# Projection matmuls grouped in threes over six PSUM banks, at the border between two token blocks

## The chip, the cores and the metric

One NeuronCore of a Trainium2 chip runs the program. The metric is the device time of one execution in microseconds (us); the kernel before was run three times and its median is what the changed kernel is held against. The engines are TensorE (PE in the profile, its weight loads PEld), VectorE (DVE), ScalarE (ACT), GpSimd (POOL) and SyncE (SP). Matmul results land in PSUM, eight banks of 128 partitions by 512 fp32.

## What is computed

A cross attention between `x` and a small `state` gives 4,352 token rows of 512 numbers; these go through a mixture of eight experts in which every expert sees every token, weighted by a matrix `P` that eight rounds of row and column normalisation make:

```
xread = softmax(scale * x @ state.T) @ state          # per batch b and head h, 512 tokens
sread = softmax(scale * state @ x.T) @ x              # 32 state rows
x     = concat(xread, sread) reshaped to (4352, 512)
for e in range(8):
    h   = max(x @ w1[e], 0)                           # 512 -> 1024
    out += P[:, e:e+1] * (h @ w2[e])                  # 1024 -> 512
```

## The kernel before

**Blocks.** The tokens are cut into nine blocks: eight of 512 tokens (one for each batch entry) and a ninth, block 8, with the 256 state rows. A first part of the program (some 140 us) computes the attention, the matrix `P` and expert 0, in an order that a small planner (`issue`, L48) writes. The rest is a loop (L858 on) over the 63 pairs of expert 1 to 7 and block 0 to 8; its order is written out by hand, and it is what the change touches. Each pair is called a block below, and written (expert, block).

**The first layer.** For a block of 512 tokens `x @ w1` is not computed from `x`. Its rows are attention weights times `state`, so `V = state @ w1` is computed first (`project`, L192, "projection"), and `hidden_ps` (L210) multiplies the attention weights `aT` by `V`. A projection of one block has two halves of 512 columns. A half is 8 matmuls that each use a 64x32 piece of the array (`tile_position`), so that all 8 stand side by side; they fill two PSUM banks, and ScalarE copies these to `V` (L208). `V` lives in a ring of three buffers. `layer1` (L226) then makes eight steps for a block; a step is one bank `hps` from two matmuls of 512 columns, which ScalarE turns into `Hm` with a relu (L238). After the fourth and the eighth step VectorE forms four sums and differences of `Hm` (L244 to L247, called S1 and S2 below). Block 8 takes its `x` from `xsT` directly, in four matmuls of 256 columns a step.

**The second layer.** `layer2` (L257) replaces the eight quarter products of `h @ w2` by seven (a Strassen scheme). Each of the seven products is 8 matmuls of 256 columns (4 in block 8), all on line 271. They go to three PSUM tiles, in this order, with k counting from 0:

- k=0: `A`; ScalarE copies it to the block's `Bseed` bank (L305)
- k=1: `E`; k=2: onto `Bseed`; k=3: onto `A`; k=4: onto `Bseed`; k=5: onto `E`; k=6: onto `Bseed`
- after each from k=1 on, VectorE adds the tile, times a column of `P`, to `acc` (`add`, L281, two instructions on L285; one in block 8). A product onto a tile waits until the add that reads the tile's former state has ended.

Two `Bseed` banks alternate between blocks.

**PSUM in the loop.** Eight banks: `A`, `E`, two `Bseed`, and a ring of four named "h", which the `hps` steps and the projections share.

**The order in the loop.** Between the products of a block come the steps of the *next* block's first layer: none after k=0 and k=1, then 1, 2, 2, 2, 1. After k=0 stands the projection of the block after the next one, both halves, wherever there is one to make: in 54 of the 63 blocks. At every sixth call of `step` a piece of the next expert's weight preparation is issued (`load_w`, L160: loads on GpSimd's queue, then eight differences `T` on VectorE, L178). In expert 1, GpSimd also multiplies `acc` by a column of `P` for each block (`weigh`, L250).

All engines run their own instructions in order, so the place at which an instruction is written in this loop is its place in its engine's queue.

Of the kernel before, what the change touches and what calls it, by code (L numbers as in the profile page):

```python
# [9 lines left out]
FP32 = mybir.dt.float32  # L10
FP16 = mybir.dt.float16
AX_X = mybir.AxisListType.X
ALU = mybir.AluOpType
AF = mybir.ActivationFunctionType
EPS = 1e-9


class Ring:
# [71 lines left out]
def kernel(  # L90
# [9 lines left out]
    nc = tc.nc  # L100
# [32 lines left out]
    def bank(shape, dtype, name, tag="bank"):  # L133
        return pools[tag].tile(shape, dtype, name=name, tag=tag)
# [20 lines left out]

    mw = ctx.enter_context(tc.tile_pool(name="moe_w", bufs=2))
    gsb = ctx.enter_context(tc.tile_pool(name="gate_sb", bufs=2))
    vpool = ctx.enter_context(tc.tile_pool(name="vpool", bufs=3))

    def load_w(e):  # L160

        w1h = mw.tile([128, NKC, F], FP16, name="w1h", tag="w1h")
        w2h = mw.tile([128, NFB, Dm], FP16, name="w2h", tag="w2h")
        w16[e] = (w1h, w2h)
        for g in range(2):
            nc.gpsimd.dma_start(out=w1h[:, ds(2 * g, 2), :], in_=w1r[e, :, ds(2 * g, 2), :])  # L166
        for g in range(2):
            nc.gpsimd.dma_start(out=w2h[:, ds(NJ * g, NJ), :], in_=w2r[e, :, ds(NJ * g, NJ), :])
        for _ in range(10):
            yield  # L170
        T = tpool[0].tile([128, 4, NJ, DH], FP16, name="T", tag="T")
        tsum[e] = T
        b11, b12 = w2h[:, :NJ, :DH], w2h[:, :NJ, DH:]
        b21, b22 = w2h[:, NJ:, :DH], w2h[:, NJ:, DH:]
        for i, (p, q) in enumerate(((b12, b11), (b22, T[:, 0]), (b22, b12), (b21, T[:, 1]))):
            for g in range(2):
                jj = ds(g * (NJ // 2), NJ // 2)
                nc.vector.tensor_sub(T[:, i, jj], p[:, jj], q[:, jj])  # L178
                yield
# [9 lines left out]
    asb = actx.enter_context(tc.tile_pool(name="attn_sb", bufs=2))  # L189
    spl = actx.enter_context(tc.tile_pool(name="stprep", bufs=1))  # L190

    def project(e, bi):  # L192
        if bi == B:
            return
        w1h = w16[e][0]
        V = vpool.tile([128, NQ, F], FP16, name="V", tag="V")
        vt[(e, bi)] = V
        for f in range(F // 512):
            cols = ds(f * 512, 512)
            ps = [bank([128, 512], FP32, "v_ps", ring[0]) for _ in range(NQ)]  # L200
            for j in range(4):
                for q in range(NQ):
                    r = ((j ^ q) % 2) * 64
                    nc.tensor.matmul(ps[q][ds(j * Ns, Ns), :], stT[ds(r, 64), bi, q, ds((j ^ q) * Ns, Ns)],  # L204
                                     w1h[ds(r, 64), 2 * q + j // 2, cols],
                                     tile_position=(r, j * Ns))
            for q in range(NQ):
                nc.scalar.copy(out=V[:, q, cols], in_=ps[q])  # L208

    def hidden_ps(e, bi, fb, out):  # L210
        w1h = w16[e][0]
# [7 lines left out]
            nc.tensor.matmul(out, lhs, rhs, start=(k == 0), stop=(k == len(terms) - 1))  # L219

    vt = {}
    ring = ["bank"]
    hid = {}
    seeds = []

# [31 lines left out]
    def layer2(e, bi, n):  # L257
        t0, tn = blocks[bi]
        nk = tn // 256
        th = tn // 2  # L260
        Hm, sm = hid.pop((e, bi))
        w2h, T = w16[e][1], tsum[e]
        tb = t0 // 128
        p = Pmat[:, :, e:e + 1]
        A = bank([128, 2, DH], FP32, "A", "A")
        Eb = bank([128, 2, DH], FP32, "E", "E")

        def product(dst, lhs, rhs, first=False):
            for c in range(nk):
                for j in range(NJ):  # L270
                    nc.tensor.matmul(dst[:, c], lhs(j, c), rhs[:, j],  # L271
                                     start=first and c == 0 and j == 0, stop=(j == NJ - 1),
                                     skip_group_check=True)

        def h(i, half):
            return lambda j, c: Hm[:, i, j, ds(half * th + c * 128, 128)]

        def s(k):
            return lambda j, c: sm[:, k, j, ds(c * 128, 128)]

        def add(src, row, col):  # L281
            for c in range(nk):
                k = tb + row * nk + c
                dst = acc[:, k, ds(col * DH, DH)]
                nc.vector.scalar_tensor_tensor(out=dst, in0=src[:, c], scalar=p[:, k], in1=dst,  # L285
                                               op0=ALU.mult, op1=ALU.add)

        def store(row):
            if e == E - 1 and bi == B:
                nb = 128 // Ns  # L290
                for i in range(nb):
                    (nc.scalar if i % 2 else nc.sync).dma_start(
                        out=outs[row * nb + i], in_=acc[ds(i * Ns, Ns), tb + row, :])

        if e == 1:
            for b in range(2) if bi == 0 else (bi + 1,):
                weigh(b)
        product(A, h(0, 0), w2h[:, :NJ, :DH], True)
        if not n:
            for i in range(2):  # L300
                bb = pb.tile([128, 2, DH], FP32, name="Bseed%d" % i)
                nc.tensor.matmul(bb.rearrange("p c d -> p (c d)"), identh, aT[:, 0, 0], start=True, stop=True)
                seeds.append(bb)
        Bb = seeds[n % 2]
        nc.scalar.copy(out=Bb[:, :nk], in_=A[:, :nk])  # L305
        yield
        product(Eb, s(0), T[:, 0], True)
        add(Eb, 1, 1)
        yield
        product(Bb, s(1), T[:, 1])  # L310
        add(Bb, 0, 1)
        yield
        product(A, h(1, 0), w2h[:, NJ:, :DH])
        add(A, 0, 0)
        yield
        product(Bb, h(0, 1), T[:, 2])
        add(Bb, 1, 1)
        yield
        product(Eb, s(2), w2h[:, NJ:, DH:])
        add(Eb, 0, 1)  # L320
        store(0)
        yield
        product(Bb, h(1, 1), T[:, 3])
        add(Bb, 1, 0)
        if e == E - 1 and bi < B:
            for k in range(2 * nk):
                nc.sync.dma_start(out=outx[bi][:, k, :], in_=acc[:, tb + k, :])
        store(1)
        yield
# [18 lines left out]
    def slot(pool, n, shape, dtype, tag):  # L348
        return Slot(rings.setdefault(tag, Ring(n)),
                    lambda: pool.tile(shape, dtype, name=tag, tag=tag))  # L350
# [333 lines left out]
    vslots = {}  # L684

    def project_ops(e, b, rank):
        V = slot(vpool, 3, [128, NQ, F], FP16, "V")
        vslots[e, b] = V
        outs_ = []
        for f in range(F // 512):  # L690
            cols = ds(f * 512, 512)
            ps = [psum([128, 512], FP32, "v_ps") for _ in range(NQ)]

            def mul(_, ps=ps, cols=cols):
                w1h = wslots[e][0].tile
                for j in range(4):
                    for q in range(NQ):
                        rr = ((j ^ q) % 2) * 64
                        nc.tensor.matmul(ps[q].tile[ds(j * Ns, Ns), :],  # L699
                                         stT[ds(rr, 64), b, q, ds((j ^ q) * Ns, Ns)],  # L700
                                         w1h[ds(rr, 64), 2 * q + j // 2, cols],
                                         tile_position=(rr, j * Ns))

            t = op(rank, {"PE": (0.40, 0.62)}, mul, stT_ready + w1_ready(e) + ([t] if f else []), ps + ([] if f else [V]), [V] if f else [])
            for q in range(NQ):
                def keep(eng, q=q, ps=ps, cols=cols):
                    copy(eng, V.tile[:, q, cols], ps[q].tile)
                    vt[e, b] = V.tile

                outs_.append(op(rank, EVICT32, keep, [t], [], [ps[q], V]))  # L710
        v_ready[e, b] = outs_
# [131 lines left out]
    for tag in ("A", "E"):  # L843
        pools[tag] = ctx.enter_context(
            tc.tile_pool(name="psum_" + tag, bufs=1, space=bass.MemoryType.PSUM))
    ring[0] = "h"
    n = 0

    def step():
# [6 lines left out]
                wload.pop(0)  # L856

    work = [(e, bi) for e in range(1, E) for bi in range(len(blocks))]  # L858
    for i, (e, bi) in enumerate(work):
        if bi == 1 and e + 1 < E:  # L860
            wload.append(load_w(e + 1))
        l2 = layer2(e, bi, i)
        l1 = layer1(*work[i + 1]) if i + 1 < len(work) and work[i + 1] not in hid else iter(())
        for k in range(7):
            next(l2)
            step()
            if k == 0 and i + 2 < len(work) and work[i + 2] not in vt:
                project(*work[i + 2])
            for _ in range((0, 0, 1, 2, 2, 2, 1)[k]):
                next(l1, None)  # L870
                step()
        for part in (l1, l2):
            for _ in part:
                pass
        if bi == len(blocks) - 3:
            for _ in (x for w in wload for x in w):
                pass
            wload.clear()
# [30 lines left out]
```

## Time and profile before

| | us |
|---|---|
| three runs: median (lowest to highest) | 768.05 (767.78 to 769.49) |
| the profiled execution's own time | 766.84 |
| its span, first to last instruction | 764.9 |
| TensorE busy | 747.9 (98%) |
| VectorE busy | 629.9 (82%) |
| ScalarE busy | 513.7 (67%) |
| GpSimd busy | 104.6 (14%) |

The profile is one execution. Its lines give an engine, a source line, the operation, what it writes and reads, the shape, a count, and times; the idle time before an instruction is given with what ended it. The end of a matmul is modelled and includes the way through the array, so matmuls that follow each other overlap in the listing: eight products of 256 columns are listed as 1.04 us and start 0.87 us before the next group. The chain view follows the last instruction back to what released it, step by step, and gives each group only the time that it adds.

### The profile page before, as it was taken

The numbers are of one execution on the slowest core, as the hardware profiler recorded it, in microseconds if no ns is written. First come the engines' busy times: TensorE is split into PE (matmuls) and PEld (weight loads), VectorE is DVE, ScalarE is ACT, GpSimd is POOL, SyncE is SP. The second block draws the span as 40 slices with busy tenths as digits, with TensorE's granted clock in tenths as the row PEclk, the third lists the DMA queues.
The fourth block names the chain that finished last, engine by engine and source line by source line (L and its number), as shares of the span: only waits on it lengthen the run. The fifth ranks groups of instructions, "written<-read, shape, count | busy, mean of one in ns | idle before, by whom it ended". The sixth has DMA issues, their size and how long they took to land.

```text
span 764.9 us, 16309 instructions
## 1 busy us (share of the span) xinstructions
PE 747.9 (98%) x6561; PEld 501.8 (66%) x6561; DVE 629.9 (82%) x1544; ACT 513.7 (67%) x1003; POOL 104.6 (14%) x102
## 2 busy tenths in 40 slices
PE   5999999999999999999999999999999999999997
PEld 3444445566776667766776767766677667766775
DVE  5998977888987888888887888888887888878886
ACT  5878976666667675766657666676657676576662
POOL 4433100799200000100001000100001000000000
PEclk9999999999999999999999999999999999999999
DMA  8997200060015000510006000240006000012234
GB/s 136 184 152 120 49 1 1 1 112 1 1 25 88 1 2 1 91 21 2 1 1 111 2 1 1 44 69 1 2 1 108 4 2 1 1 55 86 85 108 138
DMA packets 41595, 34.61 MB, mean 45 GB/s; under 512 B 16688, under 2 KB 33072, under 8 KB 41520
## 3 DMA queue, kind: packets, MB, share of 16 engines
q0 software_dynamic: 21248, 20.97, 17.7%
q1 hardware_dynamic: 19040, 12.08, 6.4%
q8 instruction: 51, 0.84, 0.4%
q10 hardware_dynamic: 1232, 0.52, 0.3%
q14 instruction: 24, 0.20, 0.1%
HBM read 42.48 MB, written 8.91 MB: 67 GB/s over the span
## 4 chain that ended last, share of the span: by engine, by line
PE 90%; DVE 5%; ACT 3%; DMA 1%; issue 0%; POOL 0%; POOLq 0%
PE hps L219 27%; PE Bseed L271 20%; PE E L271 14%; PE A L271 13%; PE yps L756 7%; PE v_ps L204 4%; PE hps L721 4%; DVE acc L285 2%; DMA x_nat<-in_x_dram 1%; DVE sm L244 1%; ACT V L357 1%; ACT Hm L238 1%; PE su_ps L596 1%; PE v_ps L699 0%; ACT xT L357 0%; PE ET_ps L581 0%
## 5 line engine op out<-in xcount | busy, mean ns | idle before, releaser
L238 ACT ACTIVATE Hm<-hps 128x512 f16<-128x512 f32 (+1 forms) x496 | 266.0, 572 | 188.5 <-PE hps L219 173.4
L219 PE MATMUL hps<-aT,V 128*128 128x512 f16 x880 | 234.8, 379 | 0.0
L271 PEld LDWEIGHTS <-Hm 128*128 128x128 f16 x1904 | 186.2, 98 | 69.8 <-issue 0.8
L285 DVE SCALAR_TENSOR_TENSOR acc<-Bseed,Pmat,acc 128x256 f32<-128x256 f32 x357 | 156.9, 479 | 56.9 <-PE Bseed L271 54.4
L271 PEld LDWEIGHTS <-sm 128*128 128x128 f16 x1428 | 134.2, 98 | 52.5 <-DVE sm L244 24.2
L271 PE MATMUL Bseed<-T,Hm 128*128 128x256 f16 x952 | 124.5, 273 | 0.4 <-DVE acc L285 0.3
L271 PE MATMUL A<-w2h,Hm 128*128 128x256 f16 x952 | 124.7, 273 | 0.0
L219 PEld LDWEIGHTS <-V 128*128 128x128 f16 x880 | 86.1, 98 | 45.2
L208 ACT CAST V<-v_ps 128x512 f16<-128x512 f32 x216 | 111.3, 610 | 0.0
L285 DVE SCALAR_TENSOR_TENSOR acc<-E,Pmat,acc 128x256 f32<-128x256 f32 x238 | 104.3, 477 | 3.7
L244 DVE TENSOR_TENSOR sm<-Hm 128x512 f16<-128x512 f16 (+1 forms) x124 | 51.7, 417 | 19.1 <-ACT Hm L238 18.3
L756 PE MATMUL yps<-w2h,hT 128*128 128x512 f16 x272 | 66.5, 380 | 0.0
L285 DVE SCALAR_TENSOR_TENSOR acc<-A,Pmat,acc 128x256 f32<-128x256 f32 x119 | 52.4, 479 | 15.8 <-PE A L271 15.7
L271 PE MATMUL E<-T,sm 128*128 128x256 f16 x476 | 64.5, 274 | 0.7
L271 PE MATMUL Bseed<-T,sm 128*128 128x256 f16 x476 | 62.4, 273 | 0.0
L271 PE MATMUL E<-w2h,sm 128*128 128x256 f16 x476 | 62.3, 273 | 0.0
L254 POOL TENSOR_SCALAR acc<-acc,Pmat 128x512 f32<-128x512 f32 x34 | 55.2, 1638 | 44.8 <-DVE Pmat L673 44.8
L166 POOL DMA_DIRECT2D w1h<-in_moe_w_dram x12 | 8.6, 721 | 355.2 <-PE hps L219 355.2
L247 DVE TENSOR_TENSOR sm<-Hm,sm 128x512 f16<-128x512 f16 (+1 forms) x124 | 53.1, 428 | 4.2
L245 DVE TENSOR_TENSOR Hm<-Hm 128x512 f16<-128x512 f16 (+1 forms) x124 | 51.6, 416 | 4.3
L246 DVE TENSOR_TENSOR sm<-sm,Hm 128x512 f16<-128x512 f16 (+1 forms) x124 | 50.0, 403 | 0.0
L305 ACT COPY Bseed<-A 128x512 f32<-128x512 f32 (+1 forms) x63 | 34.4, 546 | 18.8 <-PE A L271 17.3
(107 smaller groups left out, 554.1 us busy)
## 6 DMA issues: line engine op xcount, KB each, us to landing
w1h<-in_moe_w_dram POOLq DMA_DIRECT2D x16, 512.0 KB, 7.2
w2h<-in_moe_w_dram POOLq DMA_DIRECT2D x16, 512.0 KB, 7.5
out_dram<-acc SPq DMA_DIRECT2D x32, 256.0 KB, 2.8
x_nat<-in_x_dram POOLq DMA_DIRECT2D x16, 256.0 KB, 6.3
st_st<-in_state_dram SPq DMA_DIRECT2D x1, 256.0 KB, 4.2
st_st<-in_state_dram ACTq DMA_DIRECT2D x1, 256.0 KB, 4.6
out_dram<-acc SPq DMA_DIRECT2D x4, 64.0 KB, 1.9
out_dram<-acc ACTq DMA_DIRECT2D x4, 64.0 KB, 2.1
```

Of the source, the lines that this page charges most:

```text
L208: nc.scalar.copy(out=V[:, q, cols], in_=ps[q])
L219: nc.tensor.matmul(out, lhs, rhs, start=(k == 0), stop=(k == len(terms) - 1))
L238: nc.scalar.activation(out=Hm[:, i, j, :tn], in_=hps[:, :tn], func=AF.Relu)
L244: nc.vector.tensor_add(s1, a21, a22)
L245: nc.vector.tensor_sub(a21, a11, a21)
L246: nc.vector.tensor_sub(s2, s1, a11)
L247: nc.vector.tensor_sub(s4, a12, s2)
L254: nc.gpsimd.tensor_scalar(out=acc[:, k, :], in0=acc[:, k, :], scalar1=Pmat[:, k, 0:1], scalar2=None, op0=ALU.mult)
L271: nc.tensor.matmul(dst[:, c], lhs(j, c), rhs[:, j], start=first and c == 0 and j == 0, stop=(j == NJ - 1), skip_group_check=True)
L285: nc.vector.scalar_tensor_tensor(out=dst, in0=src[:, c], scalar=p[:, k], in1=dst, op0=ALU.mult, op1=ALU.add)
L305: nc.scalar.copy(out=Bb[:, :nk], in_=A[:, :nk])
L756: nc.tensor.matmul(yps.tile, hT[fb].tile[:, ds(tk * 128, 128)], w2h[:, fb, :], start=(fb == 0), stop=(fb == NFB - 1))
```

## The change

`project` now takes a list of three halves, which may belong to two blocks, and the block's number, and does its work as a generator in two parts. Its 24 matmuls are issued in one go. The first half goes to the `E` bank and to the `Bseed` bank of the block that follows; the other two go to the four "h" banks. ScalarE's copies of the first two banks are issued with the matmuls, those of the other four at the second call.

The loop calls it ahead of `layer2` of block i, so the matmuls stand between product k=6 of the block before and product k=0 of this one; the other four copies come after k=0, behind the copy of `A` to `Bseed`. A session is made only where the next block's `V` is not complete, which gives 36 sessions of three halves for the 54 of two. The steps of the first layer get other places: the string PAT with a session, PAT0 without, PATN in block 7 and PATS in block 8 (without a session). In all of them no step comes after k=6, and the fourth step comes before k=4.

```diff
+PAT = (0, 0, 1, 3, 2, 2, 0)
+PAT0 = (0, 1, 1, 2, 2, 2, 0)
+PATN = (1, 1, 1, 2, 2, 1, 0)
+PATS = (1, 1, 1, 1, 2, 2, 0)
+VB = 3
...
-    def project(e, bi):
-        if bi == B:
-            return
-        w1h = w16[e][0]
-        V = vpool.tile([128, NQ, F], FP16, name="V", tag="V")
-        vt[(e, bi)] = V
-        for f in range(F // 512):
+    def project(halves, n):
+        banks = []
+        for k, (e, bi, f) in enumerate(halves):
+            if (e, bi) not in vt:
+                vt[(e, bi)] = vpool.tile([128, NQ, F], FP16, name="V", tag="V")
+            w1h = w16[e][0]
             cols = ds(f * 512, 512)
-            ps = [bank([128, 512], FP32, "v_ps", ring[0]) for _ in range(NQ)]
+            if k:
+                ps = [bank([128, 512], FP32, "v_ps", "h") for _ in range(NQ)]
+            else:
+                ps = [bank([128, 512], FP32, "v_ps", "E"), seeds[n % 2].rearrange("p c d -> p (c d)")]
             for j in range(4):
                 for q in range(NQ):
                     r = ((j ^ q) % 2) * 64
                     nc.tensor.matmul(ps[q][ds(j * Ns, Ns), :], stT[ds(r, 64), bi, q, ds((j ^ q) * Ns, Ns)],
                                      w1h[ds(r, 64), 2 * q + j // 2, cols],
                                      tile_position=(r, j * Ns))
-            for q in range(NQ):
-                nc.scalar.copy(out=V[:, q, cols], in_=ps[q])
+            banks += [(vt[(e, bi)][:, q, cols], ps[q]) for q in range(NQ)]
+        for dst, src in banks[:2]:
+            nc.scalar.copy(out=dst, in_=src)
+        yield
+        for dst, src in banks[2:]:
+            nc.scalar.copy(out=dst, in_=src)
+        yield
...
+    halves = [(e, bi, f) for e, bi in work if bi < B and (e, bi) not in vt for f in range(F // 512)]
     for i, (e, bi) in enumerate(work):
         if bi == 1 and e + 1 < E:
             wload.append(load_w(e + 1))
+        v = iter(())
+        pat = PATS if bi == B else PATN if bi == B - 1 else PAT0
+        if i + 1 < len(work) and (work[i + 1] + (F // 512 - 1,)) in halves:
+            v = project(halves[:3], i)
+            pat = PAT
+            del halves[:3]
+        next(v, None)
         l2 = layer2(e, bi, i)
         l1 = layer1(*work[i + 1]) if i + 1 < len(work) and work[i + 1] not in hid else iter(())
         for k in range(7):
             next(l2)
             step()
-            if k == 0 and i + 2 < len(work) and work[i + 2] not in vt:
-                project(*work[i + 2])
-            for _ in range((0, 0, 1, 2, 2, 2, 1)[k]):
+            if k == 0:
+                next(v, None)
+            for _ in range(pat[k]):
                 next(l1, None)
                 step()
```

More of the change, by code (lines that the diff above doesn't have):

```diff
@@ L157 @@
     gsb = ctx.enter_context(tc.tile_pool(name="gate_sb", bufs=2))
-    vpool = ctx.enter_context(tc.tile_pool(name="vpool", bufs=3))
+    vpool = ctx.enter_context(tc.tile_pool(name="vpool", bufs=VB))
     def load_w(e):
@@ L221 @@
     vt = {}
-    ring = ["bank"]
     hid = {}
@@ L686, in project_ops @@
     def project_ops(e, b, rank):
-        V = slot(vpool, 3, [128, NQ, F], FP16, "V")
+        V = slot(vpool, VB, [128, NQ, F], FP16, "V")
         vslots[e, b] = V
@@ L845 @@
             tc.tile_pool(name="psum_" + tag, bufs=1, space=bass.MemoryType.PSUM))
-    ring[0] = "h"
     n = 0
```

## The prediction, made before the changed kernel was run

> **What bounds the kernel now.** I read the page first, then TensorE's busy time by windows, the chain, the timeline of some blocks, and the order of the instructions of both programs on each engine.
>
> ```profile
> PE 747.9 (98%) x6561; PEld 501.8 (66%) x6561; DVE 629.9 (82%) x1544; ACT 513.7 (67%) x1003; POOL 104.6 (14%) x102
> 300.00:450.00 150.00, 149.92 (x1303) 106.28 (x1302) 123.98 (x309) 101.40 (x195) 5.83 (x8) 1.00 0.17 29
> ```
>
> In the loop TensorE is busy 149.92 of 150 us at a granted clock of 1.00 (the second line: PE, PEld, DVE, ACT, POOL, clock). So only TensorE's own time, or a new wait of TensorE, can move the end. Its time at a projection, in the chain:
>
> ```profile
> 303.20 0.87 PE A L271 x8
> 304.07 0.56 PE v_ps L204 x16
> 304.63 0.98 PE E L271 x8
> ```
>
> A product costs 0.87 us; a session of two halves costs 0.56 and makes the next product 0.11 longer, together 0.67 (0.66 from the starts). A half streams 512 columns through eight pieces side by side, 0.215 us, as one matmul of 512 columns does (four `hps` matmuls: 0.86). So 0.66 - 0.43 = 0.23 us a session is spent on going into and out of the small pieces.
>
> **Fewer sessions.** 54 sessions become 36, the 108 halves stay: 18 x 0.23 = **4.1 us less**. That the 0.23 belongs to the session and not to its matmuls, the first part shows, where a single half stands between products:
>
> ```profile
> 112.65 1.02 PE L756 MATMUL yps<-w2h,hT 128*128 128x512 f16 x4
> 113.60 0.41 PE L699 MATMUL v_ps<-w1h,stT 64*32 64x512 f16 x8
> 113.95 1.04 PE L756 MATMUL yps<-w2h,hT 128*128 128x512 f16 x4
> ```
>
> Four matmuls end their streaming at 112.65 + 0.86 = 113.51, the next group starts at 113.95: 0.44 for one half, 0.22 of it fixed. From below, the saving could be nothing (a rival).
> A rule of the Trainium skill speaks against it: "TensorE: Matmul & The Clock Gate", section "The cost: per-tile semaphore tail", lets the tail grow with the packed matmuls and their semaphore increments. By its formula the tail would be an estimated 0.21 us for 16 matmuls with 4 increments and 0.30 for 24 with 6, so 54 and 36 of them would cost nearly the same. The trace doesn't agree: 0.22 after 8 matmuls, 0.23 after 16.
>
> **Waits that go.** Where a block has no session (block 6 of each expert), the last step of the first layer stands right before k=0, and S2 comes too late for k=1:
>
> ```profile
> 294.09 1.29 PE L271 MATMUL E<-T,sm 128*128 128x256 f16 x8
> ```
>
> 1.29 against 1.04: 0.25 us, in six experts; in (7,6) and (7,7) 0.23 each. All steps now end before k=6, so S2 has 0.87 us more. With three small ones (0.2): **2.2 us less**. In (7,8) a wait of 0.3 for S2 goes, but the next two waits for adds take its place; nothing.
>
> **Waits that come: S1.** The order shows what the diff hides: the fourth step now comes before k=4, so on VectorE S1 stands ahead of the add of k=4, which before was ahead of S1. Product k=6 waits for that add. The parts, from the timeline:
>
> ```profile
> 299.76 1.08 ACT L238 ACTIVATE Hm<-hps 128x512 f16<-128x512 f32 x2 [0.65 <-PE hps L219]
> 300.39 0.42 DVE L244 TENSOR_TENSOR sm<-Hm 128x512 f16<-128x512 f16 x1 [0.18 <-ACT Hm L238]
> 301.99 0.42 DVE L178 TENSOR_TENSOR T<-w2h,T 128x512 f16<-128x512 f16 x1
> ```
>
> S1 takes 1.60 us (300.39 to 301.99). Relus follow each other by 0.49 and last 0.59; the first starts 0.20 after its matmuls' streaming, and S1 0.03 after the relu. An add of two lasts 0.87, and TensorE starts 0.05 after it. With A's first matmul at 0, a 512-token block with a session has k=1 at 0.87, k=2 at 1.75, a step at 2.62, k=3 at 3.05, steps at 3.92, 4.36, 4.79, k=4 at 5.22, k=6 at 8.69. The relu of the fourth step: 4.56 + 2 x 0.49 = 5.54 to 6.13; S1 6.17 to 7.77; add to 8.64; k=6 may start at **8.69, the moment at which TensorE is there**. Without a session (two steps after k=3) the margin is 0.06. I take 0.01 for each of 32 session blocks, 0.3 us; the ends are 0 (a margin as worked out) and 0.15 (twice the 0.07 by which a relu right behind a copy holds ScalarE longer), 4.8 us.
>
> In expert 1 S1 is longer, while GpSimd's `weigh` runs (140 to 196 us):
>
> ```profile
> L244 DVE TENSOR_TENSOR sm<-Hm x10: 408/424/881, 150.7 to 195.6; 128x512 f16<-128x512 f16 x10
> L247 DVE TENSOR_TENSOR sm<-Hm,sm x10: 424/712/795, 152.4 to 196.9; 128x512 f16<-128x512 f16 x10
> ```
>
> (minimum/median/maximum in ns). The five S1 there take 0.3 to 0.8 more; hidden before, they now go to k=6: 5 x 0.5 = **2.4 us more** (0 if GpSimd falls elsewhere, 4.2 at 0.83 each).
> "SBUF — State Buffer", section "Who interferes with whom", of the Trainium skill says that a VectorE instruction with two SBUF inputs is fully blocked by a GpSimd one that reads SBUF; by that an S1 could wait a whole `weigh` instruction, here 1.6 us (its row's mean, 1638 ns), and an estimate for five would be 8. The largest extra in the trace, 0.8, is half of it.
>
> **Block 8 pays most.** A product there is 0.44, so the chain through S1 has less cover. ScalarE's rows:
>
> ```profile
> 314.01 0.36 ACT L305 COPY Bseed<-A 128x256 f32<-128x256 f32 x1
> 314.33 2.05 ACT L208 CAST V<-v_ps 128x512 f16<-128x512 f32 x4
> 316.24 1.64 ACT L238 ACTIVATE Hm<-hps 128x512 f16<-128x512 f32 x3
> ```
>
> With a session (experts 1, 3, 4, 6): the copy to Bseed starts 0.24 after A's streaming, 0.68 to 1.04; k=2 can start at 1.10 and would have at 0.87: 0.22 (before, the session stood between). The four V copies follow, ScalarE is free at 2.91; the first `hps` bank is free at 1.65, wanted at 1.53: 0.11. Four relus from 2.91 end at 5.05 (spacing 0.56, 0.49, 0.49 as in the last row), S1 5.08 to 6.68, one add to 7.16, k=6 at 7.21; TensorE is there at 6.41: 0.80. Together 1.13 x 4 = **4.5 us more**. Without a session (experts 2, 5): fourth relu ends at 4.27, S1 5.90, add 6.38, k=6 at 6.43 for 6.07: 0.36 x 2 = **0.7 more**. Before, none of this: 313.33 to 320.50 is the bare sum of the matmuls and a session.
>
> **What costs nothing, and its cover.** The session now needs the E bank: in a session block the add of k=5 ends at 9.42, the first small matmul would be at 9.66: 0.2 of cover; T stands ahead of that add in (3,5) and (5,5) and costs 0.1 each. The Bseed and E copies (start 0.20 after the first half) end at 0.24 and 0.73 after A starts, the copy of A to Bseed ends at 1.69, k=2 wants it at 1.75: cover 0.01 with the way to TensorE, and each later ns is paid 32 times. Behind it on ScalarE are four V copies, to 3.66; the steps that need their banks come at 2.62 and from 3.92, when they are free. The "h" banks that the session takes are free after the eighth relu, 9.6, for 9.9. The V ring stays at three: a slot's last reader is two blocks back. w1 of the next expert is loaded from 225 and 313.8 us, some 70 us ahead of its first reader; SP's stores keep their order, and T stays as many.
>
> **The sum.** -4.1 - 2.2 + 0.3 + 2.4 + 4.5 + 0.7 + 0.2 = **+1.8 us**, 766.8 to 768.6 for an execution like the profiled one (span 764.9, 1.9 around it). That one is 1.2 below the median of three, 768.05; on the median's footing 769.9.
>
> **The rivals** (on that footing).
> 1. *The gain stands alone*, not slower: the add of k=4 is not late, because S1 starts sooner than in my chain. It would have to be 0.4 sooner in blocks 8 without a session and in expert 1, 0.8 with one; from there on nothing new is paid, and 6.3 are saved: 768.05 - 6.3 = 761.8. For it: between 200 and 740 us an add holds TensorE up only three times now, by 0.03 in block 7. Against: the order puts S1 ahead of the add, and the chain's parts repeat in every block. Chance 0.15.
> 2. *Only block 8 pays*: in expert 1 GpSimd's instructions fall beside other work. -6.3 + 0.5 + 5.2: 767.5. Chance 0.17.
> 3. *The zero margin turns into a wait in every session block*, slower: if relus, copies or S1 come 0.15 later than in my chain, each of 32 blocks waits as long, at k=6 or at k=2: 769.9 + 4.5 = 774.4 (0.05 would already be 1.6). Against: the durations repeat to a few ns. Chance 0.18.
> 4. *The sessions' cost goes with their matmuls*, so the change does not save what it groups: 769.9 + 4.1 = 774.0. Against: the single halves above. Chance 0.05.
> The forecast has 0.45.
>
> **How the numbers follow.** 0.2% is 1.5 us, about what a measurement can tell from no change. The forecast at +1.8 is near that bound; uncertain by 1.5 either way, 0.28 of its 0.45 lies above and 0.17 within. Rival 2 gives 0.10 within and 0.07 faster; rival 1 is faster; 3 and 4 slower. So faster 0.22, same 0.27, slower 0.51. The range, 764.5 to 774, leaves out rival 1 and the upper half of 3. The forecast's own range is 767.5 to 772.
>
> **What would show it.** 36 groups of 24 `v_ps` matmuls in the chain, at 0.23 above their 0.65 each; the 1.29 gone; waits of TensorE for VectorE's acc before the last Bseed product: about 0.8 in four blocks 8, 0.4 in two, 0.3 to 0.8 in (1,0) to (1,4), and almost none elsewhere. I would be wrong if those adds came before S1 in time, if a session waited for the E bank, or if the ordinary session blocks, which I give 10.45 us each, took more.

## The result, and the profile after

| | median of 11 runs, us | lowest to highest |
|---|---|---|
| before | 767.79 | 766.45 to 769.77 |
| after | 770.61 | 769.33 to 772.5 |

The ratio is 1.0037, with a 95% interval of 1.0027 to 1.0048: slower by 2.8 us, or 0.37%, and so beyond the 0.2% (1.5 us) that the prediction took as the bound to no change. The forecast was 769.9, +1.8. The profiled execution took 770.73 us with a span of 768.9.

The page, and TensorE's time by windows, as they were shown of before:

```profile
PE 743.6 (97%) x6561; PEld 504.6 (66%) x6561; DVE 623.8 (81%) x1544; ACT 509.1 (66%) x1003; POOL 104.3 (14%) x102
300.00:450.00 150.00, 148.99 (x1278) 107.39 (x1277) 122.18 (x308) 98.16 (x191) 5.83 (x8) 1.00 0.18 29
```

TensorE has 4.3 us less to do in the whole program, for the same 6,561 matmuls, and yet is no longer busy all the time: 148.99 of 150 us in place of 149.92, at the same granted clock of 1.00. Work was saved and waits were bought. Both can be read from single lines. The first saving, in the timeline of block (1,6), which has no session (start, length, group):

```profile
208.65 1.04 PE L282 MATMUL A<-w2h,Hm 128*128 128x256 f16 x8
209.52 1.04 PE L282 MATMUL E<-T,sm 128*128 128x256 f16 x8
210.40 0.60 PE L231 MATMUL hps<-aT,V 128*128 128x512 f16 x2
```

Product k=1 takes the usual 1.04; where a block had no session before, the listing had 1.29. The other saving is in the sessions, here the one ahead of block (2,6); the listing gives its first eight small matmuls one by one, of which one is shown:

```profile
296.43 1.04 PE L282 MATMUL Bseed<-T,Hm 128*128 128x256 f16 x8
297.40 0.39 PE L211 MATMUL v_ps<-w1h,stT 64*32 64x512 f16 x1
...
297.62 0.62 PE L211 MATMUL v_ps<-w1h,stT 64*32 64x512 f16 x16
298.17 1.05 PE L282 MATMUL A<-w2h,Hm 128*128 128x256 f16 x8
```

From the start of the last k=6 matmul to the second matmul of A, 1.096 us pass around 24 small matmuls in 34 of 36 sessions, to within 2 ns (the two others wait for the E bank), where 0.880 passed around 16 before. Less two ordinary spacings of 0.109, a session costs 0.878 after and 0.662 before: 36 x 0.878 - 54 x 0.662 = -4.1 us.

What was bought shows in TensorE's own waits (who waited for whom: total us, times, longest):

```profile
PE Bseed L282 <- DVE acc L296: 5.6, 11, 0.9
PE Bseed L282 <- ACT Bseed L316: 0.7, 4, 0.2
```

Before, the second was not there, and the first read:

```profile
PE Bseed L271 <- DVE acc L285: 0.3, 1, 0.3
```

These waits are idle time behind matmuls whose listed ends include the way through the array; counted from start to start they are 0.16 each longer. Ten of the eleven are new: four in expert 1 and six in the blocks 8. The eleventh is the one of (7,8) that was there before; a fifth in expert 1, 0.31 from start to start in (1,3), is too short for the list. And the rows of S1 and S2 in expert 1 (minimum/median/maximum ns):

```profile
L255 DVE TENSOR_TENSOR sm<-Hm x10: 407/418/1170, 150.6 to 198.0; 128x512 f16<-128x512 f16 x10
L258 DVE TENSOR_TENSOR sm<-Hm,sm x10: 424/754/797, 151.8 to 199.2; 128x512 f16<-128x512 f16 x10
```

From the first product of the loop to the last matmul the profiled executions take 618.0 us before and 621.0 after: +3.0, for 2.8 between the medians. (The two profiled executions as wholes are 3.9 apart. The part ahead of the loop, which the change leaves as it was, took 1.0 longer in the second: the loop's first product starts at 142.4 and at 143.4.) By the start-to-start spacing of the matmuls the 3.0 divides like this, each row rounded:

| term | forecast | after, by the trace |
|---|---|---|
| sessions: 18 fewer | -4.1 | -4.1 |
| waits for S2 gone, small ones | -2.2 | -2.1 |
| k=1 of block (1,0) waits for S2 | not seen | +0.4 |
| k=6 in expert 1, (1,0) to (1,4) | +2.4 | +3.3 |
| k=6 in blocks 8 | 4 x 0.80 + 2 x 0.36 = +3.9 | 4 x 0.79 + 2 x 0.36 = +3.9 |
| k=2 and the first step in four blocks 8 | 4 x 0.33 = +1.3 | 4 x 0.39 = +1.6 |
| E bank late behind a T | +0.2 | +0.2 |
| k=6 at zero margin elsewhere | +0.3 | 0.0 |
| waits in (7,8) | 0 | -0.1 |
| sum, before rounding | +1.8 | +3.0 |

### The profile page after: what moved, and what is told of

The parts are those of the page before. It is cut to its first block, busy times and chain, and to the rows that moved or that the text cites. A ratio compares the mean times of both kernels' runs of the same rounds, so it can differ in the third digit from the quotient of the medians.

```text
span 768.9 us, 16228 instructions
## 1 busy us (share of the span) xinstructions
PE 743.6 (97%) x6561; PEld 504.6 (66%) x6561; DVE 623.8 (81%) x1544; ACT 509.1 (66%) x1003; POOL 104.3 (14%) x102
## 4 chain that ended last, share of the span: by engine, by line
PE 84%; DVE 6%; ACT 5%; DMA 3%; issue 1%; POOL 0%; POOLq 0%
PE hps L231 24%; PE Bseed L282 19%; PE A L282 13%; PE E L282 12%; PE yps L767 6%; PE v_ps L211 4%; PE hps L732 3%; ACT Hm L249 2%; DMA x_nat<-in_x_dram 2%; DVE acc L296 1%; DMA xT<-x_nat 1%; ACT V L219 1%; DVE sm L258 1%; DVE sm L255 1%; DVE Hm L256 1%; DVE sm L257 1%
## 5 line engine op out<-in xcount | busy, mean ns | idle before, releaser
L282 PEld LDWEIGHTS <-Hm 128*128 128x128 f16 x1904 | 183.1, 98 | 79.8 <-issue 24.7
L231 PE MATMUL hps<-aT,V 128*128 128x512 f16 x880 | 229.3, 379 | 0.0
L282 PEld LDWEIGHTS <-sm 128*128 128x128 f16 x1428 | 139.3, 98 | 35.0 <-issue 1.6
L219 ACT CAST V<-v_ps 128x512 f16<-128x512 f32 x144 | 74.2, 610 | 0.0
L282 PE MATMUL E<-T,sm 128*128 128x256 f16 x476 | 62.4, 273 | 0.3 <-DVE sm L839 0.3
L316 ACT COPY Bseed<-A 128x512 f32<-128x512 f32 (+1 forms) x63 | 34.4, 546 | 42.1 <-PE A L282 38.0
```

What stands on the lines that cost most here:

```text
L219: nc.scalar.copy(out=dst, in_=src)
L282: nc.tensor.matmul(dst[:, c], lhs(j, c), rhs[:, j], start=first and c == 0 and j == 0, stop=(j == NJ - 1), skip_group_check=True)
```

## The experiments

Theory A, the prediction's: the new waits are the add of k=4 standing behind S1 on VectorE. Theory B, the rival: the time goes to the new place and the banks of the sessions, and to ScalarE's copies that stand ahead of its relus.

**S1 behind the add, nothing else.** The changed kernel with one condition in `layer1`:

```diff
-                if j % 2 and i:
-                    jj = ds(j - 1, 2)
+                if (i, j) in ((0, 2), (1, 3)):
+                    jj = ds(0 if j == 2 else 2, 2)
```

> The changed kernel with one thing moved: the four instructions of S1 are issued with the fifth step, so that on VectorE they stand behind the add of k=4. TensorE's order is the same, instruction for instruction. Theory A (the new waits are the add of k=4 standing behind S1): the 7.2 us of waits before k=6 go; the add of k=5 now stands behind S1 and the session needs its bank, by my chain 0.06 us before it is wanted, so expert 1 gives back 0.2 to 1 us at three or four borders and two blocks 8 some 0.3 each. 770.6 - 7.2 + 2 = 765.5 us, between 763.5 and 767. Theory B (the time goes to the place and the banks of the sessions, with ScalarE's copies ahead of its relus): nothing moves, 770.6.

Measured: 765.7 us, ratio to before 0.9971 (0.9958 to 0.9984): faster than both kernels. TensorE's waits there:

```profile
PE v_ps L211 <- DVE acc L296: 1.9, 8, 0.4
PE Bseed L282 <- ACT Bseed L316: 0.7, 4, 0.2
PE Bseed L282 <- DVE acc L296: 0.4, 1, 0.4
```

Of the eleven waits of Bseed products for an add, one is left, the old one in (7,8). In exchange the session waits eight times for the add of k=5, which now stands behind S1 (2.5 us from start to start, of which 1.4 in expert 1; 0.2 of it was there in the changed kernel), and k=1 of (1,3) waits 0.26. That is -7.2 + 2.3 + 0.3 = -4.6, and the loop is 4.7 shorter. Theory A holds, and B falls for this part: no bank, no place and no copy was moved.

**The new places of the steps, without the sessions of three.** The kernel before, with the steps' new places in its loop:

```diff
+        two = i + 2 < len(work) and work[i + 2] not in vt and work[i + 2][1] < B
+        pat = (1, 1, 1, 2, 2, 1, 0) if bi == B - 1 else (0, 0, 1, 3, 2, 2, 0) if two else (1, 1, 1, 1, 2, 2, 0) if bi == B else (0, 1, 1, 2, 2, 2, 0)
...
-            for _ in range((0, 0, 1, 2, 2, 2, 1)[k]):
+            for _ in range(pat[k]):
```

> The kernel before, with the new places of the first layer's steps alone: sessions of two halves, after k=0, in the h banks, as they were. Theory A: the waits for S2 go (-2.2), the waits before k=6 come in expert 1 (+3.3) and in the six blocks 8 (0.5 each by the chain with ScalarE free at 2.9 us, +2.8): 767.8 + 3.9 = 771.7 us, between 770 and 773.5. Theory B: the steps alone only take the S2 waits away, 765.6.

Measured: 774.25 us, 1.0083 (1.006 to 1.0106), above both expectations. The trace names the reason, and it is the experiment's own:

```profile
217.26 0.63 PE L204 MATMUL v_ps<-w1h,stT 64*32 64x512 f16 x16
218.54 0.60 PE L219 MATMUL hps<-xsT,w1h 128*128 128x256 f16 x4 [0.65 <-ACT V L208]
218.97 0.27 PE L271 MATMUL E<-T,sm 128*128 128x256 f16 x1
```

In block 7 a step now stands right behind the projection, and all four h banks are the projection's; the step waits for ScalarE's first copy, 0.72 us from start to start, in six blocks: 4.3 us that belong to none of the theories. So the run was made again with block 7 like the others:

```diff
-        pat = (1, 1, 1, 2, 2, 1, 0) if bi == B - 1 else (0, 0, 1, 3, 2, 2, 0) if two else (1, 1, 1, 1, 2, 2, 0) if bi == B else (0, 1, 1, 2, 2, 2, 0)
+        pat = (0, 0, 1, 3, 2, 2, 0) if two else (1, 1, 1, 1, 2, 2, 0) if bi == B else (0, 1, 1, 2, 2, 2, 0)
```

> The second run without the wait that its own edit brought: there block 7 had a step right behind the projection, whose matmuls wait for an h bank that ScalarE has not copied yet (0.72 us in six blocks by its trace). Here block 7 takes the places of the other blocks with a session. Theory A: 774.25 - 4.4 = 769.9 us, 2 above the kernel before: S1 ahead of the add costs 4.7 and the S2 waits give back 2.2. Theory B: below the kernel before, 765.6.

Measured: 769.33 us, 1.0022 (1.0011 to 1.0033).

```profile
PE Bseed L271 <- DVE acc L285: 3.2, 11, 0.4
```

Here, too, k=6 waits for an add in five blocks of expert 1 and in the six blocks 8, 4.7 us from start to start (0.47 in each block 8; 1.9 in expert 1; the list leaves out the short one of (1,0) and has that of (7,8)), and the S2 waits are gone. The loss comes with the places of the steps, with the old sessions in their old banks.

**No `weigh`.** The changed kernel with `weigh(b)` left out of `layer2`:

```diff
-            for b in range(2) if bi == 0 else (bi + 1,):
-                weigh(b)
+            pass
```

> The changed kernel without GpSimd's multiplication of acc by a column of P in expert 1 (that part of the computation is left out). Theory A with GpSimd as the reason that S1 is longer in expert 1: the 3.3 us of waits in (1,0) to (1,4) fall to nearly nothing, 770.6 - 3.2 = 767.4 us. If S1 is longer there for another reason: 770.6.

Measured: 766.79 us, 3.8 below the changed kernel; 0.9986 (0.9973 to 0.9999) to before.

```profile
PE Bseed L282 <- DVE acc L296: 3.3, 7, 0.6
L255 DVE TENSOR_TENSOR sm<-Hm x10: 424/425/426, 150.6 to 195.0; 128x512 f16<-128x512 f16 x10
L258 DVE TENSOR_TENSOR sm<-Hm,sm x10: 424/425/425, 151.8 to 196.2; 128x512 f16<-128x512 f16 x10
```

Without GpSimd's work beside them the same instructions take 425 ns throughout, where they took up to 1170, and the five waits in expert 1 (3.3 us) are gone, with the 0.4 of block (1,0); the seven left are those of the six blocks 8 and of (7,8). GpSimd is the reason that S1 was longer.

**Sessions of two halves at the border.** The changed kernel with `halves[:2]` in place of `halves[:3]`, twice, which makes 54 sessions:

> The changed kernel with sessions of two halves at the border, 54 of them, in the E, Bseed and two of the h banks. If the fixed 0.23 us belongs to the session: +4.1, and some 1 us less of waits in the blocks 8, whose relus come sooner behind two copies, 0.7 each in six in place of 5.5 in all: 773.7 us. If the cost goes with the matmuls (rival 4): only the last, 769.6.

Measured: 773.53 us, 1.0068 (1.0049 to 1.0086), 2.9 above the changed kernel. Its sessions cost 0.662 us each, as before the change, in 51 of 54; the other three wait 0.14 each for the E bank. With a session ahead of each of six blocks 8 they pay 0.10 at k=1, 0.44 at k=2 and 0.47 at k=6, 6.1 in all; expert 1 pays 1.9 at k=6. So in the loop, which is 3.6 longer, it is +4.1 for the sessions, +0.6 in the blocks 8 (I had expected less there), +0.2 for the E bank and -1.4 in expert 1.

**No session ahead of a block 8.** The first experiment's kernel, with the sessions moved one block up there:

```diff
-        if i + 1 < len(work) and (work[i + 1] + (F // 512 - 1,)) in halves:
+        if i + 1 < len(work) and bi < B and (bi < B - 1 or e + 1 < E) and (work[i + 1 + (bi == B - 1)] + (F // 512 - 1,)) in halves:
```

> S1 behind the add of k=4 as in the first run, and the four sessions that stood ahead of blocks 8 now stand ahead of the blocks 7 before them (36 sessions still; block 7 with a session takes PAT). Theory A, with what is left in blocks 8 put down to the sessions there (the copy of A to Bseed waits for the V copy that reads the same bank, 0.33 and 0.07 in four blocks, and two borders that wait for the E bank, 0.27 each): 2.1 us go, 765.7 - 2.1 = 763.6 us, 0.5% below the kernel before. If the waits only move to block 7: 765.7.

Measured: 763.82 us, 0.9948 (0.9934 to 0.9961): the fastest of all, 0.5% below the kernel before and 6.8 us below the changed one. The waits in blocks 8 are gone, but for those of the last, (7,8). The session's waits for the E bank stayed at 2.6 us in all: two behind blocks 8 went, two behind a T came, since the T instructions fall elsewhere. So 1.5 us went in the loop and not 2.1.

## Why the prediction was right, and where its sizes were off

**Sessions.** Right in mechanism and size. 0.446 us can be worked out for a single half in the first part, 0.662 for two, 0.878 for three: 0.216 a half and 0.23 a session. Rival 4 is out. So is the Trainium skill's formula ("TensorE: Matmul & The Clock Gate", "The cost: per-tile semaphore tail") for this use, counted over all matmuls of a session: 16 matmuls with 4 increments and 24 with 6 left the array 0.308 us after their last start alike.

**Waits that go.** Right for S2. I missed that in block (1,0) the old session itself was the cover: two halves stood there between k=0 and k=1 while the last sums of the first part ran; without them k=1 waits 0.46 for such a sum, and a wait of 0.1 at k=2 went. With the steps moved and the old sessions kept (769.33 us) k=1 does not wait there.

**S1.** The step that decided, and it held: k=6 waits for an add that waits for S1. Block 8 of expert 1 shows the whole chain (start, us, piece):

```profile
229.50 0.36 ACT Bseed L316
229.85 1.97 ACT V L219 x4
231.83 1.98 ACT Hm L249 x4
...
233.83 0.44 DVE sm L255
...
235.08 0.42 DVE sm L258
235.51 0.41 DVE acc L296
235.91 0.04 issue
235.96 0.60 PE Bseed L282 x4
```

The copy of A, the four V copies, four relus, the four instructions of S1, the add, the product: the order that was worked out by hand, and k=6 late by 0.79 for a forecast of 0.80. Part of that closeness is luck. The prediction took 0.56 us as the time for which a relu right behind a copy holds ScalarE (its bound of 0.15 comes from there too); in the trace of before that was a wait: the next relu started 0.416 after the start of its second matmul, as relus that wait for TensorE do there. In block (1,8) after, where the matmuls of all four were long done, the relus start 0.49, 0.48 and 0.48 apart and the last takes 0.68: 2.12 in all, where the prediction's parts give 2.13. ScalarE was also free 0.07 later than worked out, because of the bank below, but that held up TensorE at k=2 by as much.

In the ordinary session blocks outside expert 1's first five, 29 of them, the margin of zero was zero: none waits at k=6 for more than 4 ns, and the add ends 58 to 66 ns ahead of k=6, where a product that waits starts 52 to 55 ns behind its add. Without a session it ends some 120 ns ahead, the 0.06 that was worked out. Rival 3 is out.

**Expert 1, the mis-sized term.** I took 0.5 us for each of five blocks; k=6 waited 0.3, 1.1, 0.8, 0.3, 0.8. I had taken the sizes from S1 as it fell before, but how long VectorE is held up depends on where its instruction falls in GpSimd's row of 1.6 us instructions, and all had moved. In (1,1):

```profile
161.17 7.04 POOL L265 TENSOR_SCALAR acc<-acc,Pmat 128x512 f32<-128x512 f32 x4
161.38 1.17 DVE L255 TENSOR_TENSOR sm<-Hm 128x512 f16<-128x512 f16 x1 [1.16 <-ACT Hm L249]
163.38 0.80 DVE L258 TENSOR_TENSOR sm<-Hm,sm 128x512 f16<-128x512 f16 x1
```

The first began 0.2 after one of GpSimd's instructions and took 1.17 for 0.42; the fourth took 0.80. Their extra, 0.75 and 0.37, is the 1.1 that k=6 waited: two instructions of one S1 were held up, one after the other. A single one was not held for a whole instruction of GpSimd: the first ended 0.2 ahead of the listed end of the one beside it, and 0.75 is about half of 1.6. So the full block for which the prediction names "SBUF — State Buffer", "Who interferes with whom", of the Trainium skill is not what this trace lists, though the profile's times of GpSimd are rough.

**k=2 in block 8** was 0.33 late and not 0.22, because of the bank: the copy of A goes to the Bseed bank that the second V copy still reads. That copy ends at 229.46 and L316 starts at 229.50. I had let it start when ScalarE could take another instruction. With no session ahead of a block 8 (763.82 us) this wait is gone.

**The rivals.** 1 (the gain alone, 761.8) and 2 (only block 8 pays, 767.5) are out by the waits in the trace. But a good part of what rival 1 asked for can be had: with S1 behind the add 765.7 was measured, and 763.8 with block 8 spared. That the loss stands clear of the bound was not foreseen: +1.8 lay just above 1.5, and what made it 3.0 were terms that the prediction had too small or not at all, +0.9 in expert 1, +0.4 in (1,0), +0.3 at k=2 of the blocks 8.

## What to carry to other kernels

Where one engine is always busy, a step moved on it is judged by the other engines' queues: list what now stands ahead of each instruction that the busy engine will wait for. A saving of a few us in 700 is undone by one add that slips behind 1.6 us of other work, and won back by moving four instructions. A chain whose parts repeat to a few ns can be added up by hand; parts that another engine's instructions hold up, as GpSimd's did here, can't, and need bounds.

## What the runs showed of the hardware

- Going into 64x32 pieces and back cost 0.23 us, whether 8, 16 or 24 matmuls stood between.
- From the end of an add on VectorE to the start of the matmul that waits for it: 52 to 55 ns, in every wait of that kind; from the end of ScalarE's copy to Bseed 50 to 52.
- In an unbroken run on ScalarE behind four copies (after, block (1,8)), relus started 0.48 to 0.49 us apart and were listed with 0.65 to 0.68, where one that starts after a pause has 0.60.
- A VectorE instruction of 0.42 us took up to 1.17 beside GpSimd's of 1.6, and 0.42 to 0.43 throughout with GpSimd's left out.
